# Each batch as one expert's unit: rows out by plain transfers, the routing table only in a branch at the end

## The chip, the cores and the metric

The kernel runs on one core of a Trainium2 chip. Its time is the device time of one execution in microseconds (us). Before the change the median of three runs is 590.32 us (589.46 to 590.48).

## The reference

Three layers, in float32, one behind the other:

```python
# 1. Nystrom attention: 4 batches, 8 heads, 576 tokens, head size 64, 32 landmarks
A, Bm, C = softmax(q k_lm), softmax(q_lm k_lm), softmax(q_lm k)
Z = pseudo-inverse of Bm by six Newton steps
attn = A @ Z @ C @ v                      # -> x[2304, 512], batch by batch
# 2. a dense layer ("moe"): 512 -> 2048 -> 512
h = x @ w_in ; y = (h * clip(h + 3, 0, 6) / 6) @ w_out
# 3. a mixture of 8 experts, one expert for each token, capacity 576 tokens
logits = y @ w_gate ; expert = argmax(logits) ; gate = max of softmax(logits)
# the first 576 tokens of each expert are kept, in order; the others give zero rows
out[token] = gate * (relu(y[token] @ w1[expert]) @ w2[expert])
```

With the inputs of the runs, the reference sends all 576 tokens of batch 0 to expert 2, all of batch 1 to expert 3, and all of batches 2 and 3 to expert 4. Expert 4 is full after batch 2, so the rows of batch 3 are zero.

## The kernel before

**Attention and the dense layer.** Tokens are held in eight blocks of 288, two for each batch. The attention's steps and the first quarter of the dense layer are put in order by hand, by a small planner in the file (class `Order`). The dense layer runs in four quarters of its inner size (`fq` 0 to 3). In each, block after block, `first` multiplies x by a quarter of w_in (six matmuls into ph) and `second` multiplies the result by w_out (twelve matmuls into py). Operands are split into a high and a low part, so that each product is three matmuls. The result y lies transposed in `yacc`: model dimension on the partitions, tokens along the row. The last two blocks (batch 3) get only their logits, by `logits`; their inner values go to DRAM (`r_d`) in case they are needed.

After the first quarter, the order on each engine is that of the framework's scheduler, which works from estimated durations; each engine and each DMA queue then runs its list strictly in order. The loop `moe_rest` goes through (fq, block), in four steps k a block; in each step it emits a `first`, a `second`, one step of the routing (`state["route"]`) and what `side` puts there.

**Routing, in the last quarter.** When a block's y is complete, `route(blk)` runs beside the next blocks: `gate_logits` (8 matmuls), `choose` (the expert of each token as one-hot `oh`, and its gate), then a running count of each expert, and a slot for each token in a table in DRAM, `tab_d` (expert times 2304 plus rank), with token number and gate as its entry. Three indirect DMAs a block on GpSimd's queue write these entries (L898). `turn_y` (L916) transposes y back into rows of tokens, four transposes for 128 rows, ScalarE copies them (L918), and SP's queue writes them to `y_d` (L920).

**The pick.** When both blocks of batch 0 are in the table, `pick` takes the expert with most tokens. SP reads its number into a register and loads its first 576 table entries (`load_idx`, L956 and L957). `gather_first` fetches those rows of y_d by indirect DMA, `turn_first` transposes them and splits them into `xT` (high and low). `w1_first` loads that expert's w1 in four parts and splits it (L994 load, L1000 ScalarE, L1003 VectorE).

**The experts' units.** A unit is up to 576 tokens of one expert. `run_unit` does an up layer (192 matmuls, L1071), and a down layer (96 matmuls on four full blocks of 128 tokens, L1090, and 16 on the last 64 tokens, L1097, which go first). Within the down layer of a unit the next one is prepared: `split1` splits its w1, `turn_rows` (L975) transposes its gathered rows, `fetch2` loads its w2 (L1053). The rows of the result are scaled by the gate and scattered to `out` by indirect DMA on GpSimd's queue (L1107). After unit 0, n_units and n_new are read into registers on all engines; a branch skips `finish_last` (batch 3, L1209), and the other units stand in nested branches (L1211). `out` and batch 3's part of y_d are cleared by writes of zeros in the second quarter (`clear`, L815).

The order of the preparations around the last quarter is one list:

```python
    AHEAD = [(4, 0, gather_first, 0), (4, 0, gather_first, 1), (4, 1, gather_first, 2), (4, 1, gather_first, 3),
             (4, 2, gather_first, 4), (4, 0, w1_first, 0), (4, 2, w1_first, 1), (5, 2, w1_first, 2), (6, 0, w1_first, 3),
             (5, 0, turn_first, 0), (5, 1, turn_first, 1), (5, 2, turn_first, 2), (5, 3, turn_first, 3), (6, 0, turn_first, 4)]
```

The first two numbers are block and step at which the call is emitted.

Of the kernel before, what the change touches and what calls it, by code (L numbers as in the profile page):

```python
# [114 lines left out]
def nystrom_moe_kernel(ctx, tc, qt, kt, v, w_in, w_out, w_gate, w1, w2, capacity, out, dims, dbg=None):  # L115
# [34 lines left out]
    if dbg:  # L150
        y_d, tab_d = dbg
# [24 lines left out]
    for e in range(E):  # L176
# [8 lines left out]
    cnt2 = kp.tile([RT, 2, E], BF16, name="cnt2")  # L185
    nc.gpsimd.memset(cnt2, 0.0)
    cnt_b = cnt2[:, 1, :]
# [3 lines left out]
    below = kp.tile([1, E, UB], F32, name="below")  # L191
    nc.gpsimd.iota(below, pattern=[[0, E], [UNIT, UB]], base=0, channel_multiplier=0,
                   allow_small_or_imprecise_dtypes=True)
    pick_i = kp.tile([1, 3], I32, name="pick_i")
# [6 lines left out]
    idx0 = kp.tile([P, NST, 2], I32, name="idx0")  # L201
    nc.gpsimd.memset(idx0, -1)
# [228 lines left out]
    def moe_rest():  # L431


        while state["todo"]:
            fq, blk = state["todo"].pop(0)
            prev, gh = state["prev"], []
            for k in range(NF):
                if blk < NBLK:
                    emit(first(fq, blk, k, gh))
                if prev and prev[1] < LAST:  # L440
                    emit(second(prev[0], prev[1], k, prev[2]))
                if prev and prev[1] >= LAST and k == 1:
                    logits(*prev)
                if prev and prev[1] >= LAST and k == 2 and prev[0] == NQ - 1:
                    ahead[prev[1]] = choose(lacc[prev[1] - LAST], prev[1])
                next(state["route"], None)
                side(fq, blk, k)
            if prev and prev[0] == NQ - 1:
# [15 lines left out]
    SIDE[1] += [(5, n, "clear", n) for n in range(4)] + [(6, n, "clear", 3 + n) for n in (1, 2)]  # L464
# [338 lines left out]
    ahead = {}  # L803
# [35 lines left out]
    def choose(lt, blk):  # L839
# [6 lines left out]
        sc = mp.tile([RT, 4, RN, 1], F32, tag="sc", name="sc", bufs=4)  # L846
        bc = [RT, RN, E]
        nc.vector.tensor_reduce(sc[:, 0], lg, axis=AX.X, op=ALU.max)
        oh = mp.tile([RT, RN, E], F32, tag="oh", name="oh", bufs=4)
# [8 lines left out]
        ent = mp.tile([RT, RN, 2], I32, tag="ent", name="ent", bufs=4)  # L858
        nc.vector.reciprocal(ent[:, :, 1:2].bitcast(F32), sc[:, 2])
        nc.gpsimd.iota(ent[:, :, 0:1], pattern=[[RT, RN]], base=blk * HB, channel_multiplier=1)  # L860
        ohb = mp.tile([RT, 2, RN, E], BF16, tag="ohb", name="ohb", bufs=4)
        nc.vector.tensor_copy(ohb[:, 0], oh)
        return sc, oh, ent, ohb

    def route(blk):
        if blk < LAST:
            lt = gate_logits(blk)
            yield
            sc, oh, ent, ohb = choose(lt, blk)
        else:  # L870
            sc, oh, ent, ohb = ahead[blk]
        bc = [RT, RN, E]
        if blk == LAST:
            nc.vector.tensor_copy(cnt2[:, 0, :], cnt_b)
        nc.vector.tensor_copy(ohb[:, 1, 0, :], cnt_b)
        for j in range(RN):
            dst = ohb[:, 1, j + 1, :] if j < RN - 1 else cnt_b
            nc.vector.tensor_tensor(dst, ohb[:, 1, j, :], ohb[:, 0, j, :], op=ALU.add)
        yield
        turn_y(blk, 0)  # L880
        if blk < LAST:
            yield
            turn_y(blk, 1)
            turn_y(blk, 2)
        ps = bank([RT, RN, E], "ps_c")
        nc.tensor.matmul(ps, lhsT=upper, rhs=ohb[:, 0], start=True, stop=False)
        nc.tensor.matmul(ps, lhsT=ones_b, rhs=ohb[:, 1], start=False, stop=True)
        t1 = mp.tile([RT, RN, E], F32, tag="t1", name="t1", bufs=4)
        nc.vector.tensor_tensor(t1, ps, oh, op=ALU.mult)
        nc.vector.tensor_reduce(sc[:, 0], t1, axis=AX.X, op=ALU.add)  # L890
        nc.vector.tensor_tensor(t1, oh, base_e[:, None, :].to_broadcast(bc), op=ALU.mult)
        nc.vector.tensor_reduce(sc[:, 1], t1, axis=AX.X, op=ALU.add)
        nc.vector.tensor_tensor(sc[:, 1], sc[:, 1], sc[:, 0], op=ALU.add)
        nc.vector.tensor_scalar(sc[:, 0], sc[:, 0], cap_f, float(E * NT), op0=ALU.is_ge, op1=ALU.mult)
        slot = mp.tile([RT, RN], I32, tag="slot", name="slot", bufs=4)
        nc.vector.tensor_tensor(slot, sc[:, 1, :, 0], sc[:, 0, :, 0], op=ALU.add)  # L896
        for j in range(RN):
            ins = nc.gpsimd.indirect_dma_start(  # L898
                tab_d, bass.IndirectOffsetOnAxis(ap=slot[:, j:j + 1].bitcast(U32), axis=0),
                ent[:, j, :], None, bounds_check=E * NT - 1, oob_is_err=False)  # L900
            for other in placed:
                tc.declare_no_dep(ins.ins, other.ins, reason="every token has a slot of its own")
            placed.append(ins)
        if blk == NBLK // B - 1:
            pick()

    def turn_y(blk, j):

        t = blk % 2 * 2 + j
        n = min(P, S - t * P)  # L910
        if blk >= LAST or blk % 2 == 0 and j == RN - 1:
            return
        t0 = blk // 2 % 2 * S + t * P
        ps = bank([P, KC, P], "ps_r")
        for d in range(KC):
            nc.tensor.transpose(ps[0:n, d, :], yacc[blk // 4][d][:, t0:t0 + n], ident)  # L916
        yr = mp.tile([P, DM], F32, tag="yr", name="yr", bufs=3)
        nc.scalar.activation(yr[0:n, :], ps[0:n].rearrange("p d c -> p (d c)"), AF.Copy)  # L918
        t0 += blk // 4 * 4 * HB
        nc.sync.dma_start(y_d[t0:t0 + n, :], yr[0:n, :])  # L920

    def pick():

        ps = bank([RT, E], "ps_k")
        nc.tensor.matmul(ps, lhsT=ones_b, rhs=cnt_b, start=True, stop=True)
        key = mp.tile([1, E], F32, name="pk", bufs=1)
        nc.vector.scalar_tensor_tensor(key, ps[0:1, :], float(E), rank[:, 0:E], op0=ALU.mult, op1=ALU.add)
        top = mp.tile([1, 8], F32, name="pt", bufs=1)
        nc.vector.max(top, key)
        nc.vector.tensor_copy(pick_i[:, 0:1], top[:, 0:1])  # L930
        nc.vector.tensor_scalar(pick_i[:, 2:3], pick_i[:, 0:1], E.bit_length() - 1, None,
                                op0=ALU.logical_shift_right)
        nc.vector.tensor_scalar(pick_i[:, 0:1], pick_i[:, 0:1], E - 1, None, op0=ALU.bitwise_and)
        nc.vector.tensor_scalar(pick_i[:, 1:2], pick_i[:, 0:1], float(NT), None, op0=ALU.mult)
        ex, sl = (nc.values_load(pick_i[0:1, n:n + 1], engines=[ET.SP], min_val=0, max_val=m,
                                 skip_runtime_bounds_check_because=ON_CHIP) for n, m in ((0, E - 1), (1, (E - 1) * NT)))
        state["ex"] = ex
        load_idx(idx0, sl)
        state["src"] = rows_of(idx0, mp.tile([P, NST], I32, name="src0", bufs=1))

        seen = mp.tile([1, 2], F32, name="seen", bufs=1)
        lead = mp.tile([1, NCAND], F32, name="lead", bufs=1)
        nc.vector.tensor_scalar(seen[:, 0:1], pick_i[:, 0:1], float(UB), None, op0=ALU.mult)
        nc.vector.tensor_scalar(lead, rank, seen[:, 0:1], None, op0=ALU.is_equal)
        nc.vector.tensor_copy(seen[:, 0:1], pick_i[:, 2:3])
        nc.vector.tensor_scalar(seen[:, 1:2], seen[:, 0:1], float(UNIT), float(NT), op0=ALU.is_ge, op1=ALU.mult)
        nc.vector.tensor_tensor(seen[:, 0:1], seen[:, 0:1], seen[:, 1:2], op=ALU.max)
        belowf = below.rearrange("p e u -> p (e u)")
        nc.vector.scalar_tensor_tensor(belowf, lead, seen[:, 0:1], belowf, op0=ALU.mult, op1=ALU.add)

    tail = UNIT - (NST - 1) * P
    xT = [t.rearrange("p g n -> p (g n)").rearrange("p (k n) -> p k n", k=KC) for t in at[0]]

    def load_idx(ti, sl):
        full = (NST - 1) * P
# [301 lines left out]
```

## Time and profile before

| | |
|---|---|
| median of three runs | 590.32 us |
| the profiled execution | 589.89 us, span 588.1 us |
| busy: PE / DVE / ACT / POOL | 565.2 / 302.9 / 306.8 / 252.0 us |
| PE's matmuls of the dense layer (L362, L400) | 133.3 + 160.6 + 114.4 us |
| PE's matmuls of the experts (L1071, L1090, L1097) | 26.9 + 25.8 + 25.7 + 69.5 + 11.0 us |
| PE's last matmul ends | 576.75 us |
| DMA | 71.27 MB |

The engines are named PE (TensorE matmul), PEld (TensorE weight load), DVE (VectorE), ACT (ScalarE), POOL (GpSimd) and SP, whose queue issues most of the DMAs. The ends of matmuls are modelled and overlap, so busy times of PE rows cannot be added up; the distance from one start to the next can.

### The profile page before, as it was taken

The page shows a single profiled execution, that of the slowest core. Times are in us where ns is not written, and L with a number is a line of the kernel's source. Part 1 is how long each engine was busy: PE and PEld are TensorE (multiplying, and loading weights), DVE is VectorE, ACT ScalarE, POOL GpSimd, SP SyncE. Part 2 cuts the span into 40 slices and gives each one's busy share as a digit, 9 for nine tenths or more (in the row PEclk, how much of TensorE's full clock was granted, in tenths as well). Part 3 has the DMA queues.
Part 4 walks back from the last instruction along what each step waited for, and adds up shares of the span by engine and source line. Part 5 has one row for each costly group of instructions (what it writes and reads, how often), then busy time and mean ns, then how long its engine had stood idle before and what let it go on. Part 6 is the DMA issues. An engine that isn't in the chain of part 4 may idle for free. (4 is left out here: it accounts for less than half of the span.)

```text
span 588.1 us, 12087 instructions
## 1 busy us (share of the span) xinstructions
PE 565.2 (96%) x4606; PEld 483.2 (82%) x4606; DVE 302.9 (52%) x837; ACT 306.8 (52%) x706; POOL 252.0 (43%) x287
## 2 busy tenths in 40 slices
PE   8999999999999999999999999899999999999992
PEld 7767678797777999879998899798997797899771
DVE  2779987633555575555655766577642022202120
ACT  3779778654675654456544544454355155343520
POOL 3467647633052532134420012332698275647630
PEclk9999999999999999999999999999999999999997
DMA  7757254004781232112302001543756143416511
GB/s 294 253 191 280 115 194 120 32 1 118 250 270 38 82 99 90 64 37 72 103 17 71 2 37 46 181 134 100 191 191 193 58 162 102 151 54 199 169 47 40
DMA packets 31354, 71.27 MB, mean 121 GB/s; under 512 B 6704, under 2 KB 11312, under 8 KB 31280
## 3 DMA queue, kind: packets, MB, share of 16 engines
q1 hardware_dynamic: 27248, 61.89, 31.7%
q0 software_dynamic: 3392, 8.42, 4.9%
q8 instruction: 40, 0.66, 0.5%
q14 instruction: 34, 0.28, 0.2%
q10 hardware_dynamic: 640, 0.02, 0.1%
HBM read 52.46 MB, written 17.86 MB: 120 GB/s over the span
## 5 line engine op out<-in xcount | busy, mean ns | idle before, releaser
L400 PE MATMUL py<-ghi,wo 128*128 128x288 f32 x768 | 160.6, 301 | 3.1 <-ACT ghi L381 2.1
L362 PE MATMUL ph<-at,vv 128*128 128x288 f32 x768 | 133.3, 309 | 0.1
L400 PEld LDWEIGHTS py<-ghi,wo 128*128 128x128 f32 x768 | 124.3, 189 | 5.7 <-ACT ghi L381 2.3
L362 PEld LDWEIGHTS ph<-at,vv 128*128 128x128 f32 x768 | 108.3, 189 | 20.2 <-issue 17.7
L400 PE MATMUL py<-glo,wo 128*128 128x288 f32 x384 | 114.4, 298 | 0.7 <-DVE glo L385 0.2
L385 POOL TENSOR_TENSOR glo<-r,ghi 128x288 fp32r<-128x288 f32 x72 | 58.2, 810 | 108.0 <-ACT ghi L381 92.4
L371 ACT ACTIVATE r<-ph,half 128x288 f32<-128x288 f32 x128 | 64.0, 500 | 54.8 <-PE ph L362 45.9
L373 DVE SCALAR_TENSOR_TENSOR r<-r,ph 128x288 f32<-128x288 f32 x128 | 57.6, 450 | 43.7 <-ACT r L371 43.2
L400 PEld LDWEIGHTS py<-glo,wo 128*128 128x128 f32 x384 | 72.6, 189 | 1.8 <-POOL glo L385 1.1
L1090 PE MATMUL ps_o<-w2s,hT 128*128 128x512 f32 x288 | 69.5, 395 | 0.0
L1090 PEld LDWEIGHTS ps_o<-w2s,hT 128*128 128x128 f32 x288 | 53.2, 188 | 13.1 <-issue 2.4
L381 ACT ACTIVATE ghi<-r 128x288 fp32r<-128x288 f32 x96 | 42.4, 442 | 38.1 <-DVE r L373 37.7
L1077 DVE SCALAR_TENSOR_TENSOR hT<-ps_h,hT 128x288 fp32r<-128x288 f32 x48 | 21.9, 456 | 78.4 <-ACT hT L1074 51.7
L898 POOL DMA_INDIRECT tab_d<-ent,slot x24 | 22.4, 935 | 83.8 <-DVE slot L896 45.5
L411 DVE TENSOR_TENSOR yacc<-py,yacc 128x288 f32<-128x288 f32 x72 | 32.6, 453 | 18.8 <-PE py L400 18.6
L1074 ACT ACTIVATE hT<-ps_h 128x288 fp32r<-128x288 f32 x48 | 19.6, 408 | 39.9 <-PE ps_h L1071 38.9
L1102 ACT ACTIVATE rows_o<-ps_o,idx 128x512 f32<-128x512 f32 x12 | 8.3, 688 | 46.8 <-PE ps_o L1090 37.3
L1107 POOL DMA_INDIRECT out<-rows_o,idx x15 | 14.7, 982 | 41.0 <-ACT rows_o L1102 26.5
L272 POOL TENSOR_TENSOR wo<-cvt,wo 128x512 fp32r<-128x512 f32 x16 | 20.6, 1288 | 25.1 <-ACT wo L270 25.1
L1037 POOL TENSOR_TENSOR w2s<-raw,w2s 128x512 fp32r<-128x512 f32 x24 | 30.1, 1293 | 1.7 <-ACT w2s L1036 1.7
L726 PE MATMUL pn<-yy 128*128 128x192 f32 (+1 forms) x112 | 28.2, 334 | 0.4 <-DVE st L654 0.2
L1071 PE MATMUL ps_h<-at,vv 128*128 128x288 f32 x192 | 26.9, 297 | 0.0
(268 smaller groups left out, 931.7 us busy)
## 6 DMA issues: line engine op xcount, KB each, us to landing
raw<-in_moe_w SPq DMA_DIRECT2D x12, 1024.0 KB, 6.9
raw<-in_moe_w_in SPq DMA_DIRECT2D x16, 512.0 KB, 6.0
raw<-in_moe_w_out SPq DMA_DIRECT2D x16, 512.0 KB, 3.8
out<-zero SPq DMA_DIRECT2D x6, 768.0 KB, 5.6
r_d<-r SPq DMA_DIRECT2D x32, 144.0 KB, 1.8
vm<-in_v SPq DMA_DIRECT2D x8, 512.0 KB, 7.3
qT<-in_q SPq DMA_DIRECT2D x6, 576.0 KB, 6.9
qT<-in_k SPq DMA_DIRECT2D x6, 576.0 KB, 6.5
```

The source lines that it names most:

```text
L362: nc.tensor.matmul(ph, lhsT=vv[pair][g][a][:, b, f * P:(f + 1) * P], rhs=at[pair][c][:, g, tok], start=n == 0, stop=n == 3 * NG - 1)
L371: nc.scalar.activation(r, ph, AF.Relu, bias=half, scale=1.0 / 6.0)
L373: nc.vector.scalar_tensor_tensor(r, r, 1.0, ph, op0=ALU.min, op1=ALU.mult)
L381: nc.scalar.activation(ghi, r, AF.Copy)
L385: eng.tensor_tensor(glo, r, ghi.bitcast(F32), op=ALU.subtract)
L400: nc.tensor.matmul(py, lhsT=w[a][:, f, d * P:(d + 1) * P], rhs=gh[f][c], start=f == 0 and n == 0, stop=f == NF - 1 and n == 2)
L411: nc.vector.tensor_tensor(y, py, y, op=ALU.add)
L726: nc.tensor.matmul(pn[:, cols], lhsT=yy[:, 0:P], rhs=yy[:, cols], start=True, stop=True)
L898: ins = nc.gpsimd.indirect_dma_start(tab_d, bass.IndirectOffsetOnAxis(ap=slot[:, j:j + 1].bitcast(U32), axis=0), ent[:, j, :], None, bound ...
L1037: nc.gpsimd.tensor_tensor(dst[1], src, dst[0].bitcast(F32), op=ALU.subtract)
L1071: nc.tensor.matmul(ps, lhsT=w1s[i % 2](f // NF, a, kk)[:, fs], rhs=xT[c][:, kk, cols], start=n == 0, stop=n == 3 * KC - 1)
L1090: nc.tensor.matmul(ps, lhsT=hT[a][:, f, cols], rhs=w2s[c][:, f, :], start=n == 0, stop=n == 3 * FC - 1)
```

## The change

Batches 0 to 2 are each taken as one unit, in order of tokens, on the assumption that each batch has chosen one expert. Then the unit's x is the batch's y as it lies, transposed, in `yacc`: it is written to DRAM in that form (`yt_d`) and loaded again for units 1 and 2; for unit 0 it is split straight out of `yacc` (`x_first`). The gates go through DRAM (`gate_d`) to come back with tokens on the partitions. Rows of `out` are contiguous and written by plain DMAs on SP's queue. `count(b)` takes each batch's counts and picks its expert, one register on SP each. `plain` works out whether the assumption holds (each of batches 0 to 2 has one expert, all different, batch 3 goes to one of them, capacity 576). If not, a branch at the very end clears `out`, builds the table, turns y back into rows and runs the general units.

```diff
-    SIDE[1] += [(5, n, "clear", n) for n in range(4)] + [(6, n, "clear", 3 + n) for n in (1, 2)]
+    SIDE[1] += [(5, n, "clear", n) for n in range(2)]
...
-    fill = mp.tile([P, E * NT // P, 2], I32, name="fill", bufs=1)
-    nc.gpsimd.memset(fill[:, :, 0:1], -1)
-    nc.gpsimd.memset(fill[:, :, 1:2], 0)
-    nc.gpsimd.dma_start(tab_d.rearrange("(p n) t -> p n t", p=P), fill)
...
-        parts = [r.rearrange("(p n) d -> p n d", p=RT) for r in (out, y_d[LAST * HB:, :])]
-        for r, k in zip(parts, (NT // RT // 6, S // RT // 6)):
-            nc.sync.dma_start(r[:, n * k:(n + 1) * k, :], zero[0:RT, None, :].to_broadcast([RT, k, DM]))
+        r = out[LAST * HB:, :].rearrange("(p n) d -> p n d", p=RT)
+        k = S // RT // 2
+        nc.sync.dma_start(r[:, n * k:(n + 1) * k, :], zero[0:RT, None, :].to_broadcast([RT, k, DM]))
...
+        nc.vector.reciprocal(prob[:, blk], sc[:, 2])
+        if blk < LAST:
+            nc.sync.dma_start(gate_d[blk * HB:(blk + 1) * HB].rearrange("(j p) -> p j", p=RT), prob[:, blk, :, 0])
+        if blk % 2:
+            count(blk // 2)
 
     def route(blk):
...
+        lt = gate_logits(blk)
+        if blk % 2:
+            for d in range(KC):
+                b = blk // 2
+                nc.sync.dma_start(yt_d[b, d], yacc[b // 2][d][:, b % 2 * S:(b % 2 + 1) * S])
         yield
-        turn_y(blk, 0)
-        if blk < LAST:
-            yield
-            turn_y(blk, 1)
-            turn_y(blk, 2)
-        ps = bank([RT, RN, E], "ps_c")
...
+        choose(lt, blk)
+
+    def count(b):
+
+        part = mp.tile([RT, E], BF16, tag="cnt", name="cnt", bufs=2)
+        sums = mp.tile([RT, E], F32, tag="cnt_f", name="cnt_f", bufs=2)
+        nc.vector.tensor_reduce(sums, chosen[:, 2 * b:2 * b + 2].rearrange("p b j e -> p e b j"), axis=AX.XY, op=ALU.add)
+        nc.vector.tensor_copy(part, sums)
+        ps = bank([RT, E], "ps_k")
+        nc.tensor.matmul(ps, lhsT=ones_b, rhs=part, start=True, stop=True)
+        nc.vector.tensor_copy(tot[:, b, :], ps[0:1, :])
+        if b == B - 1:
             return
...
+        state["ex", b] = nc.values_load(pick_i[0:1, b:b + 1], engines=[ET.SP], min_val=0, max_val=E - 1,
+                                        skip_runtime_bounds_check_because=ON_CHIP)
...
+    def split_x(d, src):
+        nc.scalar.activation(xT[0][:, d, :], src, AF.Copy)
+        nc.vector.tensor_tensor(xT[1][:, d, :], src, xT[0][:, d, :].bitcast(F32), op=ALU.subtract)
+
+    def x_first(d):
+        split_x(d, yacc[0][d][:, 0:S])
...
+    AHEAD = [(4, 0, w1_first, 0), (4, 2, w1_first, 1), (5, 2, w1_first, 2), (6, 0, w1_first, 3),
+             (5, 0, x_first, 0), (5, 1, x_first, 1), (5, 2, x_first, 2), (5, 3, x_first, 3)]
...
         def fetch(i):
...
             for a in range(2):
-                nc.sync.dma_start(raw1[a], w1[bass.ds(ex, 1), a * 2 * P:(a + 1) * 2 * P, :].rearrange(
-                    "o (k p) f -> p (o k) f", p=P))
-            return ex
+                load_w1(state["ex", i], a)
+            nc.sync.dma_start(xraw, yt_d[i].rearrange("k p n -> p k n"))
...
+        def load_gates(i):
+            g = gate_d[i * S:(i + 1) * S]
+            nc.sync.dma_start(gates[i][:, 0:NST - 1], g[0:full].rearrange("(t p) -> p t", p=P))
+            nc.sync.dma_start(gates[i][0:tail, NST - 1:NST], g[full:].rearrange("(t p) -> p t", p=tail))
...
-            nc.gpsimd.indirect_dma_start(out, bass.IndirectOffsetOnAxis(
-                ap=ti[0:r, t, 0:1].bitcast(U32), axis=0), ro[0:r, :], None, bounds_check=NT - 1, oob_is_err=False)
+            put(ro[0:r, :])
 
         def run_unit(i):
-            more = i < NU
+            more = i < B - 2
             if more and i:
-                ex = fetch(i + 1)
+                fetch(i + 1)
+            load_gates(i)
             for f in range(FC):
                 hi, lo = up_layer(i, f)
                 split2(f)
                 if i == 0 and f < 3:
                     with tc.issue_after(hi):
-                        fetch2(state["ex"], (f + 1,), 4)
+                        fetch2(state["ex", 0], (f + 1,), 4)
                 if i == 0 and f == 2:
-                    ex = fetch(i + 1)
-                if more and f == (3 if i else 5):
-                    with tc.issue_after(lo):
-                        src = rows_of(idx[(i + 1) % 2], up.tile([P, NST], I32, name=f"src{i + 1}"))
-                    state["src"] = src
-                    for t in range(NST):
-                        gather(t, rows_x[t], src, NT)
+                    fetch(i + 1)
             for t in range(NST):
-                down_layer(i, NST - 1 - t)
+                k = NST - 1 - t
+                rows = slice(i * S + k * P, i * S + k * P + size(k))
+                down_layer(k, gates[i][0:size(k), k:k + 1], lambda ro: nc.sync.dma_start(out[rows, :], ro))
...
                 if more and t == 1:
-                    turn_rows()
-
-        def turn_rows():
-            for n in range(NST):
-                turn(n, rows_x[n], px_p.tile([P, KC, P], F32, tag="x", name="ps_x"))
+                    for d in range(KC):
+                        split_x(d, xraw[:, d, :])
...
+        redo = up.tile([1, 1], I32, name="redo")
+        plain(redo)
+        fetch2(state["ex", 0], (0,), 4)
+        for i in range(B - 1):
+            run_unit(i)
+        again = nc.values_load(redo, min_val=0, max_val=1, skip_runtime_bounds_check_because=ON_CHIP)
+        with ExitStack() as nest:
+            nest.enter_context(tc.If(again > 0))
+            blank()
+            cnt_b = place()
+            for b in range(B - 1):
+                turn_back(b)
             finish_last()
...
             for i in range(NU):
                 nest.enter_context(tc.If(n_units > i))
-                run_unit(i + 1)
+                general(i, plan)
```

## Rows read from the trace of the kernel before

**Rows 1.** The page's first part: busy us (share of the span) x instructions, for PE.

```profile
PE 565.2 (96%) x4606; PEld 483.2 (82%) x4606; DVE 302.9 (52%) x837; ACT 306.8 (52%) x706; POOL 252.0 (43%) x287
```

**Rows 2.** Waits of PE: engine, line, waited for: us in total, times, longest.

```profile
PE py L400 <- ACT ghi L381: 2.1, 1, 2.1
...
PE ps_h L1071 <- ACTq L1209: 1.2, 1, 1.2
```

**Rows 3.** Windows: busy us of each engine, clock, DMA share, GB/s; last quarter, first unit.

```profile
core 0: us, PE busy (x) PEld busy (x) DVE busy (x) ACT busy (x) POOL busy (x), PEclk, DMA share, GB/s
340.00:412.28 72.28, 68.83 (x532) 63.18 (x529) 49.52 (x220) 35.77 (x79) 20.04 (x26) 0.98 0.32 104
412.28:465.00 52.72, 52.72 (x330) 45.10 (x330) 19.40 (x81) 21.97 (x52) 36.78 (x35) 1.00 0.57 167
```

**Rows 4.** DMA issues: line, engine, count, KB each, median us to landing.

```profile
raw<-in_moe_w SPq DMA_DIRECT2D x12, 1024.0 KB, 6.9
...
y_d<-yr SPq DMA_DIRECT2D x12, 256.0 KB, 2.8
...
idx<-tab_d SPq DMA_DIRECT2D x4, 4.0 KB, 2.0
```

**Rows 5.** Timeline of PE, starts of rounds: start us, us, engine, line, operation.

```profile
300.01 0.95 PE L362 MATMUL ph<-at,vv 128*128 128x288 f32 x6
...
302.40 0.95 PE L362 MATMUL ph<-at,vv 128*128 128x288 f32 x6
...
345.57 1.04 PE L362 MATMUL ph<-at,vv 128*128 128x288 f32 x6
...
348.55 1.04 PE L362 MATMUL ph<-at,vv 128*128 128x288 f32 x6
...
354.47 1.04 PE L362 MATMUL ph<-at,vv 128*128 128x288 f32 x6
...
357.28 1.04 PE L362 MATMUL ph<-at,vv 128*128 128x288 f32 x6
```

**Rows 6.** Groups of PE by shape: count, busy us, mean ns; transposes of turn_rows.

```profile
L975 PE MATMUL ps_x<-ident,rows_x 128*128 128x128 f32 x48 | 6.9, 276 | 0.0
```

**Rows 7.** Timeline of PE: the second unit's down layer, the third's first matmul.

```profile
498.38 5.76 PE L1090 MATMUL ps_o<-w2s,hT 128*128 128x512 f32 x24
...
508.70 14.37 PE L1090 MATMUL ps_o<-w2s,hT 128*128 128x512 f32 x62
522.91 7.31 PE L1071 MATMUL ps_h<-at,vv 128*128 128x288 f32 x54
```

**Rows 8.** Timelines of PE, ACT and SP, and one window, around the pick.

```profile
372.70 1.03 PE L362 MATMUL ph<-at,vv 128*128 128x288 f32 x6
...
378.71 0.69 PE L833 MATMUL pb<-yacc,gate 128*32 128x288 f32 x8
...
383.76 0.49 PE L843 MATMUL pb<-ident,lt 128*96 128x128 f32 x3
384.00 1.04 PE L362 MATMUL ph<-at,vv 128*128 128x288 f32 x6
...
376.48 0.63 ACT L1000 ACTIVATE wo<-raw_e 128x512 fp32r<-128x512 f32 x1 [5.12 <-DMA raw_e<-in_moe_w]
...
370.59 0.43 SPq L956 DMA_DIRECT2D idx<-tab_d  x1
...
372.30 0.88 SPq L994 DMA_DIRECT2D raw_e<-in_moe_w  x2
...
380.00:382.00 2.00, 2.00 (x10) 2.00 (x10) 1.93 (x8) 2.00 (x5) 0.88 (x2) 0.50 0.83 238
```

**Rows 9.** Timeline of PE: the last wait of the routing.

```profile
412.21 0.17 PE L886 MATMUL pb<-ohb,upper 96*96 96x24 bf16 x1 [0.73 <-ACT yr L918]
```

**Rows 10.** Timelines of ACT and POOL: the last eviction and the last scatter.

```profile
576.84 0.69 ACT L1102 ACTIVATE rows_o<-ps_o,idx 128x512 f32<-128x512 f32 x1 [4.75 <-PEq L1211]
...
577.80 0.97 POOL L1107 DMA_INDIRECT out<-rows_o,idx  x1 [4.46 <-ACT rows_o L1102]
```

**Rows 11.** Waits of SP's queue: line, waited for: us in total, times, longest.

```profile
SPq L1053 <- PE ps_o L1097: 54.4, 6, 21.3
```

More of the change, by code (lines that the diff above doesn't have):

```diff
@@ L857, in choose @@
         nc.vector.tensor_scalar(sc[:, 2], sc[:, 2], 1e-9, None, op0=ALU.add)
[L858 to L863, printed above, removed]
-    def route(blk):
-        if blk < LAST:
-            lt = gate_logits(blk)
-            yield
[L869 to L878, printed above, removed]
-        yield
-        turn_y(blk, 0)
-        if blk < LAST:
-            yield
-            turn_y(blk, 1)
-            turn_y(blk, 2)
-        ps = bank([RT, RN, E], "ps_c")
[L886 to L911, printed above, removed]
-            return
[L913 to L928, printed above, removed]
-        nc.vector.max(top, key)
[L930 to L949, printed above, removed]
@@ L1029, in nystrom_moe_kernel @@
         raw1 = [up.tile([P, 2, F2], F32, name=f"raw1{i}") for i in range(2)]
-        rows_x = [up.tile([P, DM], F32, name=f"rows_x{t}") for t in range(NST)]
-        idx1 = up.tile([P, NST, 2], I32, name="idx1")
-        nc.gpsimd.memset(idx1, -1)
-        idx = [idx0, idx1]
+        rx = up.tile([P, NST * DM], F32, name="rx")
+        rows_x = [rx[:, t * DM:(t + 1) * DM] for t in range(NST)]
+        xraw = rx[:, 0:KC * S].rearrange("p (k n) -> p k n", k=KC)
+        gates = [up.tile([P, NST], F32, name=f"gate{i}") for i in range(B - 1)]
         def split(dst, src):
@@ L1079, in up_layer, with down_layer @@
             return hi.ins, lo.ins
-        def down_layer(i, t):
-            ti = idx[i % 2]
+        def down_layer(t, gate, put):
             r = size(t)
@@ L1172, in finish_last, with turn_back @@
                     nc.sync.dma_start(y_d[blk * HB + t:blk * HB + t + n, :], rows_o[1][0:n, :])
+        def turn_back(b):
+            nc.sync.dma_start(xraw, yt_d[b].rearrange("k p n -> p k n"))
             for t in range(NST):
-                gather(t, rows_x[t], state["src"], NT)
-            turn_rows()
-        ps = px_p.tile([RT, 2, E], F32, tag="x", name="ps_n")
-        nc.tensor.matmul(ps, lhsT=ones_b, rhs=cnt2, start=True, stop=True)
-        cnt12 = up.tile([1, 2, E, 1], F32, name="cnt12")
@@ new lines, in general @@
+        def general(i, plan):
+            ex = nc.values_load(plan[0:1, 1, i:i + 1], engines=[ET.SP], min_val=0, max_val=E - 1,
+                                skip_runtime_bounds_check_because=ON_CHIP)
+            sl = nc.values_load(plan[0:1, 2, i:i + 1], engines=[ET.SP], min_val=0, max_val=E * NT - UNIT,
+                                skip_runtime_bounds_check_because=ON_CHIP)
+            nc.sync.dma_start(idx[:, 0:NST - 1, :], tab_d[bass.ds(sl, full), :].rearrange("(t p) c -> p t c", p=P))
+            nc.sync.dma_start(idx[0:tail, NST - 1, :], tab_d[bass.ds(sl + full, tail), :])
+            nc.vector.tensor_scalar(src, idx[:, :, 0], 0.0, None, op0=ALU.max)
+            for a in range(2):
+                load_w1(ex, a)
+            fetch2(ex)
+            for t in range(NST):
+                r = size(t)
+                nc.gpsimd.indirect_dma_start(rows_x[t][0:r, :], None, y_d, bass.IndirectOffsetOnAxis(
+                    ap=src[0:r, t:t + 1].bitcast(U32), axis=0), bounds_check=NT - 1, oob_is_err=False)
+                turn(t, rows_x[t])
+            for kk in range(KC):
+                split1(1, kk)
+            for f in range(FC):
+                up_layer(1, f)
+                split2(f)
+            for t in range(NST):
+                r = size(t)
+                down_layer(t, idx[0:r, t, 1:2].bitcast(F32), lambda ro: nc.gpsimd.indirect_dma_start(
+                    out, bass.IndirectOffsetOnAxis(ap=idx[0:r, t, 0:1].bitcast(U32), axis=0), ro, None,
+                    bounds_check=NT - 1, oob_is_err=False))
```

204 lines of the change are left out of this document (125 added, 79 removed).

## Prediction

> **What bounds the kernel now.** I read the page's busy times first: PE is busy 565.2 of 588.1 us [rows 1]. Then PE's own list of waits: the longest is 2.1 us, the next that matters 1.2 us [rows 2]. So nothing but TensorE's own stream sets the end. What takes an instruction out of that stream moves the end by its place in the stream; what is done on VectorE, ScalarE, GpSimd or by DMA counts only where PE waits for it. In the last quarter of the first MoE (340 to 412 us), where most of the edits fall, DVE is busy 49.5 and ACT 35.8 of 72.3 us [rows 3]: room there, not plenty. I then read PE's order of time around each piece that goes, because the matmuls overlap and a busy time is not a price: the price is start to start.
>
> **What goes from PE's stream.**
> - turn_y: 15 groups of four transposes (12 full and 3 partial blocks of rows, as the writes of y show [rows 4]). A plain round of the last quarter (six ph and twelve py matmuls) is 302.40 - 300.01 = 2.39 us, one with such a group 357.28 - 354.47 = 2.81 [rows 5]. So 0.42 us a group, 6.3 us in all.
> - turn_first: 5 groups of the same shape, 2.1 us at the same price.
> - turn_rows: 15 groups, among the down layer's matmuls (48 of the transposes, in 12 groups, are in one row [rows 6]; three groups are smaller). Between the first full down matmul of the second unit and the next unit's first matmul lie 522.91 - 498.38 = 24.53 us; it holds 96 matmuls of (522.91 - 508.70) / 62 = 0.229 us, 21.98 in all [rows 7]. The other 2.55 us are the five groups. The third unit turns rows for a fourth that never runs, so three times: 7.65 us.
> - The table's count: 8 pairs of small matmuls. A round with one group and one pair is 348.55 - 345.57 = 2.98 us, 0.17 over that with the group alone [rows 5]: 1.4 us. Two single ones (L925, L1179) go and four come in count(): 0.2 back. Net 1.2 us.
>
> **Waits that go.**
> - The pick. PE needs 384.00 - 372.70 = 11.30 us for two rounds [rows 8]. Their content: two plain rounds (4.78), the gate logits (0.69 at most), one turn_first group (0.42, already counted) and three transposes (384.00 - 383.76 = 0.24), 6.13 in all. 5.2 us are lost. The rows show how: idx waits for the table's scatters and is issued at 370.59, the first of w1 at 372.30; ACT has the split of w1 next in its queue and stands 5.12 us until 376.48; ghi is behind it, PE behind ghi [rows 2, 8]. Afterwards TensorE runs at half its clock: 0.50 granted from 380 to 382, that is 1.2 instead of 2.4 GHz [rows 8]. The change takes the expert two steps earlier (in choose, not at the end of route), from the counts alone; no table, no idx. The pick then stands two rounds (2.4 to 2.8 us each [rows 5]) earlier in PE's order, and with the table's wait gone I estimate w1's issue some 10 us before 372.30. What is late next: the four writes of yt (1.2 MB) go ahead of w1 on the same queue; at the 2.8 us of a 256 KB write [rows 4], overlapping, I estimate 4 us. That leaves the load before ACT's place for it. I take all 5.2 us; ends 0 and 5.2.
> - The end of that stage: PE waits 0.73 us for the last yr [rows 9]. It goes: 0.7. Next come the first unit's matmuls, whose x and w1 are split earlier.
> - The branch after the first unit: 1.2 us [rows 2]. The three units are straight code now: 1.2.
> - The end: after the last eviction (576.84 + 0.69) POOL needs until 577.80 + 0.97 = 578.77 for the scatter's descriptors [rows 10]; SP's issue of a plain transfer takes some 0.4 us, by that of idx (0.43) [rows 8]. 0.8 us gained, against a register load and a branch which now stand behind that write: 0 to 1.2 us by the branch wait [rows 2]. I take 0.4; ends -0.4 and 0.8.
>
> **What is added, at nothing, and its cover.**
> - Splitting x by rows of y: 4 ACT copies and 4 DVE subtractions of 128x576 a unit, from SBUF, in place of 5 and 5 of 128x512 from PSUM. With the 15 yr copies of ACT gone and some 60 tiny DVE operations of the table too, both engines get lighter [rows 3]. ACT sets no wait in the down layers, so 4 times about 0.7 us stand beside 24 us of matmuls. Uncovered: 2.8 us a unit, 8.4 in all.
> - SP's queue. It gets 12 yt writes (288 KB each) for 15 y writes, 6 writes and 6 loads of gates in 4-byte pieces (nearest: idx, 8-byte pieces, 2.0 us to landing [rows 4]), two x loads of 1.2 MB, and the 15 row writes that POOL issued; it loses idx and most of the clearing (6 of 768 KB and 6 of 192 KB become two of 576 KB). Moved past it: three register loads, one for each unit, each waiting for DVE's pick; behind them stand r_d writes (7 buffers) and w1. PE waits for none of these before. Bounds: -1 us (less traffic for the conversions) to +5.2 (one more stop like the pick's). I take 0, as no PE wait in the list is for SP.
> - POOL loses 24 scatters, 20 gathers and 15 scatters; its splits of w2 no longer queue behind them. No PE wait rests on them: 0.
>
> **The sum.** 6.3 + 2.1 + 7.65 + 1.2 + 5.2 + 0.7 + 1.2 + 0.4 = 24.75 us. The profiled execution took 589.89 us (span 588.1), so 565.1; the median of the runs is 0.43 above it: 565.5 us.
>
> **Rivals.**
> - A stop like the pick's remains or comes anew: ACT works its list in order, as ghi behind the split showed, the list is fixed ahead from estimated landings, and 1.2 MB of yt or x now share the queue with w1. For it: it happened once here [rows 8]. Against: the chain is two hops shorter. With it 570.7, and with the end and branch terms lost too, 573.
> - Two such stops, or loads late for one unit (w1 and x behind a wait on SP): some 10 us: 575 to 580.
> - Slower: SP becomes the one queue for everything the units need and give, and it is in order. Before, it stood 54.4 us in six waits for raw2, up to 21.3 at a time [rows 11], with nothing urgent behind. If the w1 and x loads of units two and three fall behind such a wait, each unit starts after 6.9 + 6.9 us of w1 [rows 4] and about 8 us of x, exposed: twice 22, so 565.5 + 44 = 609 us. It decides from 12.4 us a unit on (24.75 / 2). Against: the loads stand in program order ahead of w2's, with a whole unit's 50 us to land. The Trainium skill, page "DMA: Bandwidth & Descriptors", section "Anatomy of one DMA — SWDGE (gpsimd) path", has the rule behind this: a DMA's semaphore wait is held on the issuing sequencer, not in the DMA engines, so a waiting issue stops every later one of its engine. The trace agrees, as the wait stands on SP's queue. By the rule alone the row writes and loads would queue behind w2's wait, 609 at worst; without it 565.5.
> - It doesn't do what it says: the branch is taken. Then the three units run again with gathers, at least 3 x 52.7 us (the first unit's window [rows 3]): 565.5 + 158, over 720 us. It is taken when a batch's tokens choose more than one expert. Against: the kernel before runs three units for three batches and turns rows three times [rows 6]; and by the reference, batches 0 to 2 of the inputs go whole to experts 2, 3 and 4, and batch 3 to expert 4 again.
>
> **How the numbers follow.** Forecast (560 to 569) 0.62; one stop (569 to 574) 0.20; two stops or a late load (574 to 588) 0.10; SP blocks, slower 0.04; branch taken 0.01; more than I count 0.03: the 20 transposes among ph and py at 0.51 as in the down layer (2.55 / 5) give 1.8 more, and less DMA traffic 1, so 562.7, and below 560 only with something unseen. The range 560 to 574 leaves out 0.18. Faster by over 0.2% (1.2 us, about what can be told from no change here) 0.94, within it 0.01, slower 0.05.
>
> **What the profile after would show.** No transposes of y or x in PE's stream, only those of the logits; three units' down layers of 22.0 us plus the tail with no gap between units; PE clock 1.00 through the last quarter and no wait of ACT on raw_e; row writes on SP's queue; the last matmul's end 24 us before 577. Wrong would be: a PE wait over 1 us on xT, w1 or hT, a clock of 0.50 anywhere before the end, POOL scatters in the units, or groups of transposes that cost PE less than 0.42 us because the weight loads, not the matmuls, set the pace.

## The result and the profile after

| | before | after |
|---|---|---|
| median of four runs | 590.14 us (589.46 to 590.48) | 571.85 us (566.87 to 572.95) |
| profiled execution | 589.89 us, span 588.1 | 566.87 us, span 565.1 |
| first matmul of the first down layer | 439.71 us | 431.12 us |
| PE's last matmul ends | 576.75 us | 558.84 us |

The ratio is 0.967 [0.962, 0.972]: faster. The median lies 18.3 us under that of before, the profiled execution, the shortest of the four, 23.0 us; the forecast was 24.75. One execution of the changed kernel (751 us) and one of before (3062 us) among the runs below were in a slow state and are left out of every figure. The time is inside the range of 560 to 574, but the median is not where the forecast had it (560 to 569): it is in the stretch of the rival "one stop like the pick's remains" (569 to 574).

The profiled execution splits at the two marks of the table. PE's timelines show the first one, in before and in after:

```profile
439.71 3.65 PE L1097 MATMUL ps_o<-raw,h_tail 128*64 128x512 f32 x16
```

```profile
431.12 3.65 PE L1007 MATMUL ps_o<-raw,h_tail 128*64 128x512 f32 x16
```

| stretch | forecast gain | measured |
|---|---|---|
| to the first down layer (turn_y, turn_first, count, pick, edge) | 15.5 | 439.71 - 431.12 = 8.6 |
| down layers and branch (turn_rows 7.65, branch 1.2) | 8.85 | 17.91 - 8.59 = 9.3 |
| behind the last matmul | 0.4 | (588.1 - 576.75) - (565.1 - 558.84) = 5.1 |
| sum | 24.75 | 23.0 |

Two errors of opposite sign, then, some 7 us and some 5 us, and a middle that holds. The first part of the page of after (as [rows 1]) shows what left: PE is busy 17.7 us less, POOL 69 us less.

```profile
PE 547.5 (97%) x4452; PEld 467.6 (83%) x4452; DVE 286.0 (51%) x737; ACT 293.7 (52%) x675; POOL 183.2 (32%) x205
```

The chain of work that ended last in after (start, duration, what) is PE alone through the units: each down layer takes 22.0 us, where 24.53 stood [rows 7], and the next unit's first matmul begins where the last one of the unit before ends. No transposes and no branch are left there.

```profile
431.19 3.58 PE ps_o L1007 x16
434.77 22.01 PE ps_o L1000 x96
456.78 25.43 PE ps_h L982 x192
482.22 3.58 PE ps_o L1007 x16
485.80 22.00 PE ps_o L1000 x96
507.80 25.43 PE ps_h L982 x192
533.24 3.58 PE ps_o L1007 x16
536.82 22.02 PE ps_o L1000 x96
```

The list of PE's waits of after (as [rows 2]): the branch wait (1.2) and the wait for yr [rows 9] are gone, the long one on ghi is still there.

```profile
PE py L395 <- ACT ghi L376: 2.3, 1, 2.3
...
PE py L395 <- DVE yacc L406: 0.9, 1, 0.9
```

What makes ghi late is the splits of w1, as before [rows 8]. ACT's timeline of after has them (start, duration, operation, in brackets the idle time before it and its releaser):

```profile
366.98 0.63 ACT L909 ACTIVATE wo<-raw_e 128x512 fp32r<-128x512 f32 x1 [3.29 <-DMA raw_e<-in_moe_w]
...
384.84 0.63 ACT L909 ACTIVATE wo<-raw_e 128x512 fp32r<-128x512 f32 x1 [4.55 <-DMA raw_e<-in_moe_w]
...
390.91 0.63 ACT L909 ACTIVATE wo<-raw_e 128x512 fp32r<-128x512 f32 x1 [3.69 <-DMA raw_e<-in_moe_w]
```

SP's timeline of after shows that this is no late issue: the first of w1 goes out at 359.87 us, 12.4 earlier than before [rows 8]; some 10 were forecast.

```profile
345.74 0.32 SPq L850 DMA_DIRECT2D gate_d<-prob  x1
...
356.49 0.32 SPq L850 DMA_DIRECT2D gate_d<-prob  x1
359.87 0.97 SPq L903 DMA_DIRECT2D raw_e<-in_moe_w  x2
...
372.24 0.38 SPq L850 DMA_DIRECT2D gate_d<-prob  x1
373.78 0.32 SPq L859 DMA_DIRECT2D yt_d<-yacc  x1
376.25 0.34 SPq L903 DMA_DIRECT2D raw_e<-in_moe_w  x1
379.96 0.32 SPq L850 DMA_DIRECT2D gate_d<-prob  x1
381.44 0.34 SPq L903 DMA_DIRECT2D raw_e<-in_moe_w  x1
```

It is a slow landing. The answers for the tile raw_e (w1 as it arrives) of before, then of after; the first line of each says who waited (us, times):

```profile
  ACT wo L1000: 5.5, 2
...
DMA to landing us min/median/max: 3.7/3.9/4.9
```

```profile
  ACT wo L909: 11.8, 4
...
DMA to landing us min/median/max: 7.1/7.7/9.4
```

The windows of after (columns as in [rows 3]) show the DMA engines 65 to 97% busy where they move 33 to 55 GB/s, and then the stop: PE is busy 0.58 and 1.12 us of two 2-us windows, and the granted clock falls to 0.50, that is 1.2 of 2.4 GHz.

```profile
360.00:365.00 5.00, 5.00 (x43) 4.37 (x42) 2.22 (x6) 1.83 (x4) 0.00 (x0) 1.00 0.65 33
375.00:380.00 5.00, 5.00 (x40) 5.00 (x39) 4.29 (x19) 2.85 (x7) 0.00 (x0) 1.00 0.97 55
384.00:386.00 2.00, 0.58 (x5) 0.35 (x3) 0.11 (x1) 1.02 (x2) 0.00 (x0) 1.00 1.16 209
386.00:388.00 2.00, 1.12 (x3) 0.59 (x3) 2.00 (x8) 0.83 (x2) 0.00 (x0) 0.79 0.35 12
388.00:390.00 2.00, 2.00 (x12) 1.06 (x12) 0.59 (x2) 0.00 (x0) 0.00 (x0) 0.50 0.46 150
```

By starts of rounds on PE, the stops cost 3.57 - 2.39 = 1.2 us (367.24 to 370.81) and 10.10 - 5.64 = 4.5 us (382.43 to 392.53, where two plain rounds, the gate logits and three transposes take 4.78 + 0.62 + 0.24): 5.6 us.

At the end the last eviction starts at 558.91 us and the program is over 6.19 us later; before, 588.1 - 576.84 = 11.3. There the engines run the program's last instructions, which the profile lists under the kernel's last line (L1253 before, L1274 after). One of them is a DRAIN on GpSimd's queue: at 582.3 us it took 4971 ns before, and the longest of three took 93 ns after (min/median/max in ns, first and last start in us).

```profile
L1253 POOLq DRAIN  x1: 4971/4971/4971, 582.3 to 582.3; - x1
```

```profile
L1274 POOLq DRAIN  x3: 40/50/93, 514.6 to 564.9; - x3
```

### The profile page after: what moved, and what is told of

Its sections match the earlier page's. It is cut to its first block, busy times and chain, and to the rows that moved or that the text cites. A ratio compares the mean times of both kernels' runs of the same rounds, so it can differ in the third digit from the quotient of the medians.

```text
span 565.1 us, 11331 instructions
## 1 busy us (share of the span) xinstructions
PE 547.5 (97%) x4452; PEld 467.6 (83%) x4452; DVE 286.0 (51%) x737; ACT 293.7 (52%) x675; POOL 183.2 (32%) x205
## 2 busy tenths in 40 slices
DMA packets 27886, 59.70 MB, mean 106 GB/s; under 512 B 6576, under 2 KB 11184, under 8 KB 27824
## 4 chain that ended last, share of the span: by engine, by line
PE 79%; DMA 5%; DVE 5%; issue 5%; ACT 3%; POOL 1%; SPq 0%; POOLq 0%; ACTq 0%; DVEq 0%
PE py L395 21%; PE ph L357 14%; PE ps_h L982 14%; PE ps_o L1000 12%; DMA raw_e<-in_moe_w 3%; PE pn L721 3%; PE ps_f L538 2%; PE pb L336 2%; PE ps_o L1007 2%; PE ps_v L336 1%; POOL glo L380 1%; PE pw L704 1%; DMA cap_i<-in_moe_capacity 1%; PE pb L573 1%; DMA raw<-in_moe_w_out 1%
## 5 line engine op out<-in xcount | busy, mean ns | idle before, releaser
L357 PE MATMUL ph<-at,vv 128*128 128x288 f32 x768 | 131.7, 307 | 0.1
L1000 PE MATMUL ps_o<-w2s,hT 128*128 128x512 f32 x288 | 66.2, 391 | 0.0
L1011 ACT ACTIVATE rows_o<-ps_o,gate 128x512 f32<-128x512 f32 x12 | 8.3, 690 | 41.6 <-PE ps_o L1000 39.2
L982 PEld LDWEIGHTS ps_h<-at,vv 128*128 128x128 f32 x192 | 25.7, 188 | 0.7 <-issue 0.7
L982 PE MATMUL ps_h<-at,wo 128*128 128x288 f32 x192 | 25.8, 294 | 0.0
```

Source lines behind the costliest of these rows:

```text
L357: nc.tensor.matmul(ph, lhsT=vv[pair][g][a][:, b, f * P:(f + 1) * P], rhs=at[pair][c][:, g, tok], start=n == 0, stop=n == 3 * NG - 1)
L982: nc.tensor.matmul(ps, lhsT=w1s[i % 2](f // NF, a, kk)[:, fs], rhs=xT[c][:, kk, cols], start=n == 0, stop=n == 3 * KC - 1)
L1000: nc.tensor.matmul(ps, lhsT=hT[a][:, f, cols], rhs=w2s[c][:, f, :], start=n == 0, stop=n == 3 * FC - 1)
```

## Experiments

The theory after the result: the six gate writes, 288 pieces of 4 bytes each, keep the DMA engines at work, so w1 lands late and ACT stands at its split; the stretch at the end was GpSimd's drain after the scatters. The rivals: the yt writes ahead of w1 do it; the queue does it; ACT's order alone does it; any GpSimd transfer costs the drain. The kernel before took 590 us on the chips of the result and of e5 to e8, and 600 on those of e1 to e4 and of e9 to e12, while after took 572 on one of either kind; so variants of after are compared with after by their medians, also across chips. One mark, the start of the first down layer, says nearly all: from it to the end of the span are 134.0 us in after and 134.0 to 134.3 in every variant of after but e8, whose end was changed.

**e1: the changed kernel again.**

> The changed kernel once more, for the spread of its executions and a second trace. Theory (gate writes): executions spread over 567 to 573 us, and the longer ones lose their time between 355 and 407 us, where ACT stands for the load of w1 (3.3 + 4.6 + 3.7 us in the first trace) and PE behind it; the rest of the time is as before to 0.5 us. Rival (yt writes): the same spread, same place. Rival (something in the units or at the end): a longer execution would have a PE wait there or a longer stretch after PE's last matmul (6.3 us in the first trace).

Median 572.36 us (566.69 to 573.0), ratio 0.951 [0.947, 0.954]. The profile is of the execution of 566.69, with w1 landing after 6.9/7.5/9.1 us. So 567 is the short case, seen once in each of the two sets, and 572 the usual one.

**e2: no gates.**

```diff
-            nc.sync.dma_start(gate_d[blk * HB:(blk + 1) * HB].rearrange("(j p) -> p j", p=RT), prob[:, blk, :, 0])
...
-            g = gate_d[i * S:(i + 1) * S]
-            nc.sync.dma_start(gates[i][:, 0:NST - 1], g[0:full].rearrange("(t p) -> p t", p=P))
-            nc.sync.dma_start(gates[i][0:tail, NST - 1:NST], g[full:].rearrange("(t p) -> p t", p=tail))
+            nc.gpsimd.memset(gates[i], 1.0)
```

> Leaves out the gates: neither written to DRAM nor loaded, the rows are scaled by 1. Theory (six gate writes of 288 pieces of 4 bytes fill the DMA engines for 6.6 to 12 us each, and w1's loads behind them land after 7.1 to 9.4 us instead of 3.9): landing of w1 back to about 4 us, no stop of ACT over 1 us on it, no stretch at half clock in the last quarter, 5 to 6 us less than the fastest execution of the changed kernel, 561 us, and a spread under 1 us. Rival (the 1.2 MB of yt on the same queue): w1 still lands after 6 us or more, the stops stay, 566 to 572. Rival (the order of ACT's list alone): w1 lands after 4 us but a stop of 2 us or more stays, 564 or more.

561.22 us (560.9 to 561.86), ratio 0.934 [0.931, 0.936]: 11 us under after, and the spread of 6 us is gone with it. The tile raw_e again:

```profile
  ACT wo L907: 0.8, 1
...
DMA to landing us min/median/max: 3.3/3.6/4.3
```

The first down layer starts at 425.27, so the first stretch gains 14.4 of the forecast's 15.5. The gates' transfers are the cause; writes or loads, and by what means, is left to e5, e9 and e10. The windows tell what they do: from 360 to 365 us the DMA engines are 74% busy here and move 267 GB/s, against 65% and 33 GB/s in after.

**e3: batch 0's yt left out** (no unit reads it).

```diff
-        if blk % 2:
+        if blk % 2 and blk > 1:
             for d in range(KC):
                 b = blk // 2
```

> Leaves out the four yt writes of batch 0, which only the branch at the end would read. Theory (gate writes): w1 still lands after 7 us or more, within 1.5 us of the changed kernel. Rival (yt writes): these four writes are the ones in front of the first w1 loads; without them landing at about 4 us, the first stop (3.3 us of ACT) gone, 1.5 to 3 us less.

572.25 us (568.86 to 572.97), w1 landing after 7.0/7.5/12.7: no different from after. This rival falls for batch 0; the other yt writes stay here, but they stay in e2 too, where w1 is not late. The profile is of an execution of 572.97 us and shows what the usual, long one is: the last w1 part comes so late that ACT stands 8.24 us (3.69 in after's profile), PE's list of waits has 5.3 us behind it, and the clock is at 0.50 when it goes on. ACT's timeline, PE's waits and the windows of e3:

```profile
394.42 0.63 ACT L909 ACTIVATE wo<-raw_e 128x512 fp32r<-128x512 f32 x1 [8.24 <-DMA raw_e<-in_moe_w]
```

```profile
PE pb L833 <- ACT lt L826: 5.3, 1, 5.3
```

```profile
392.00:394.00 2.00, 0.00 (x0) 0.00 (x0) 0.00 (x0) 0.00 (x0) 0.00 (x0) 0.74 0.41 149
394.00:396.00 2.00, 0.60 (x4) 0.58 (x4) 0.92 (x2) 1.32 (x3) 0.00 (x0) 0.50 0.25 96
```

**e4: the gates moved on the chip**, by matmuls with a shifted unit matrix, nine one-column products a batch.

```diff
-            nc.sync.dma_start(gate_d[...], prob[:, blk, :, 0])
...
+            nc.tensor.matmul(ps[:, t:t + 1], lhsT=wide[:, RT - off:RT - off + P], rhs=prob[:, 2 * b + c // RN, c % RN, :],
+                             start=c == mine[0], stop=c == mine[-1])
+        nc.vector.tensor_copy(gates_k[:, b, :], ps)
```

> The whole computation, with the gates moved to their partitions on the chip: nine matmuls of one column for each batch with shifted unit matrices, one copy, no gate in DRAM. Theory (gate writes): as without gates, plus 27 one-column matmuls (by ps_k's 0.15 to 0.4 us in the stream, 2 to 4 us in all unless they run together): 562 to 565 us, spread under 1 us, faster than both kernels. Rival (yt writes or ACT's order): 568 to 575, the stops stay and the matmuls come on top.

571.69 us (568.4 to 573.3): missed. The load was mended (w1 lands after 3.2/3.6/5.3 us, ACT stands 1.8 us at it), but the nine products are 18 instructions and take 2.15 us in PE's own stream for each of the first two batches; those of the third stand in pieces among other matmuls. The clock fell too: it averaged 0.83 from 380 to 390 us, where PE was busy 9.90 us and the second batch's products stand, but stayed at 1.00 around the first batch's. What made it fall is not separated. PE's timeline and the windows of e4:

```profile
356.34 2.15 PE L873 MATMUL pb<-prob,wide 96*128 96x1 f32 x18
...
380.65 2.15 PE L873 MATMUL pb<-prob,wide 96*128 96x1 f32 x18
```

```profile
350.00:360.00 10.00, 9.88 (x81) 9.08 (x80) 5.50 (x26) 3.76 (x9) 0.00 (x0) 1.00 0.02 9
...
380.00:390.00 10.00, 9.90 (x69) 9.10 (x68) 5.33 (x19) 3.39 (x7) 0.00 (x0) 0.83 0.19 67
```

**e5: the gates written in rows.** One transpose of all gates [96 x 18] at batch 2, one copy, one write of 18 pieces of 384 bytes; the loads stay in 4-byte pieces.

```diff
-            nc.sync.dma_start(gate_d[...], prob[:, blk, :, 0])
+    def send_gates():
+        ps = bank([(B - 1) * S // RT, RT], "ps_gr")
+        nc.tensor.transpose(ps, prob[:, 0:LAST].rearrange("p b j o -> p (b j o)"), ident[0:RT, 0:RT])
+        gt = mp.tile([(B - 1) * S // RT, RT], F32, name="gt", bufs=1)
+        nc.scalar.activation(gt, ps, AF.Copy)
+        nc.sync.dma_start(gate_d.rearrange("(c p) -> c p", p=RT), gt)
```

> The whole computation: the six gate writes of 4-byte pieces become one transpose of the 96 x 18 gates, one copy and one write of 18 pieces of 384 bytes; the gate loads stay as they are. Theory (gate writes): landing of w1 about 4 us as without gates, no stop, 561 to 562.5 us, spread under 1 us; faster than both kernels. Rival (the gate loads in 4-byte pieces matter too): w2 or w1 of the units land late, PE waits over 1 us in the first unit, 564 or more. Rival (any PE work near the stage's end costs more than itself, as the one-column matmuls did): 565 or more.

562.53 us (561.75 to 563.28), ratio to before on its chip 0.952 [0.951, 0.954]; by medians 0.984 of after, and all of the computation is there. w1 lands after 3.5/4.0/4.5 us; ACT still stands 2.1 us at it, with no wait of PE behind, and the spread is 1.5 us where under 1 was expected. So it is the writes, not the loads: these stay, and in after they are issued from 406.19 us on, behind all of w1.

That it is the pieces and not the bytes does not follow from e5 alone, which changes two things: its one write is in longer pieces, and it is issued at 400.38 us, behind all of w1's loads (360.94 to 381.16), where three of after's six writes stand beside them. A write in rows beside the loads was not tried. For the pieces speak the windows named at e2, and that four yt writes of 288 KB issued between the loads of e2 (from 362.41 us) leave w1 at 3.3 to 4.3 us. DMA issues of after, then of e5 (KB each, median us to landing):

```profile
raw_e<-in_moe_w SPq DMA_DIRECT2D x4, 512.0 KB, 7.7
...
gate_d<-prob SPq DMA_DIRECT2D x6, 1.1 KB, 8.3
```

```profile
raw_e<-in_moe_w SPq DMA_DIRECT2D x4, 512.0 KB, 4.0
...
gate_d<-gt SPq DMA_DIRECT2D x1, 6.8 KB
```

The Trainium skill, page "DMA: Bandwidth & Descriptors", section "Rules for kernel authors", says that a last dimension which is strided is turned into one descriptor per element, and to make it contiguous. The profiles agree: after has 6576 packets under 512 B and e2 2928, and of the 3648 between them the elements of the six writes and six loads would be 3456. 1.1 KB in such elements took 8.3 us to land, twice what 512 KB take in e5.

**e6: before, on e5's chip.**

> The kernel before once more, for a trace of the executions of 600 us that it has shown since. Theory (its stop at w1's load and the half clock behind it have no fixed length): the extra 10 us lie between 340 and 420 us, as longer or more stops of ACT or PE there. Rival (another place): they lie in the first 340 us, in the units or after PE's last matmul.

591.93 us, clock 0.989, the shape of before: nothing on the 600 us.

**e7: before with plain row writes on SP** (the rows of units 2 and 3 change places).

```diff
-            nc.gpsimd.indirect_dma_start(out, bass.IndirectOffsetOnAxis(
-                ap=ti[0:r, t, 0:1].bitcast(U32), axis=0), ro[0:r, :], None, bounds_check=NT - 1, oob_is_err=False)
+            row = min(i, B - 1) * S + t * P
+            nc.sync.dma_start(out[row:row + r, :], ro[0:r, :])
```

> The kernel before with one part of the change alone: a unit's rows go out by plain writes on SP's queue, batch after batch, instead of scatters on GpSimd's. Theory (the 11.35 us after PE's last matmul hold GpSimd's drain of its last scatter, 5 us at the program's end): that stretch falls to about 6.5 us, as in the changed kernel (6.3), and the time by 4 to 5 us. Rival (the stretch is the nested branches' jumps): it stays at 10.5 to 11.5 us and the time falls by 0.8 us at most.

584.89 us against 590.48, ratio 0.991 [0.989, 0.992]: 5.6 us. From the last eviction (577.54) to the end are 6.4 us. A long drain is still there, but it starts at 562.8 us and is over while matmuls still run (to 577.5).

```profile
L1253 POOLq DRAIN  x1: 3746/3746/3746, 562.8 to 562.8; - x1
```

**e8: after, with the last unit's rows as plain writes on GpSimd's queue.**

```diff
-    lambda ro: nc.sync.dma_start(out[rows, :], ro))
+    lambda ro: (nc.gpsimd if i == B - 2 else nc.sync).dma_start(out[rows, :], ro))
```

> The changed kernel with the last unit's five row writes as plain writes on GpSimd's queue. Theory (drain of GpSimd's queue at the end after any late DMA of it): the stretch after PE's last matmul grows from 6.3 to about 11 us, the time by 4 to 5 us. Rival (only indirect DMAs cost that): it grows by 1 us at most.

572.52 us, from the last eviction (559.40) to the end 6.9 us, 0.7 more than in after; longest drain 474 ns. A plain transfer on GpSimd's queue does not bring the drain back. The long drains are in the kernels with indirect transfers (before, e7); no run took these out of before and left the rest, so what makes the drain long is open.

```profile
L1274 POOLq DRAIN  x3: 44/107/474, 564.8 to 566.0; - x3
```

**e9: after, with ACT's part of every split of w1 held in program order**, so that none stands early in ACT's list. The writes stay.

```diff
-                if n == 0:
-                    tc.keep_in_program_order(ins)
+                tc.keep_in_program_order(ins)
```

> The changed kernel with all of w1's splits on ACT kept where the program puts them, three steps behind their loads (before, only every other one was), the gate writes as they are. Theory (a late load costs only where ACT has its split early in its list): w1 still lands after 7 us or more, the ACT stops of 3 to 8 us mostly go, 561 to 564 us, small spread. Rival (the load comes so late, or the DMA engines are so filled, that something else stops): 567 to 573 with the same spread.

562.44 us (561.8 to 565.42, a wider spread than e5's), ratio 0.935 [0.930, 0.940]. w1 lands as late as in after, and nobody on ACT waits for it:

```profile
  DVE vv L911: 1.6, 2
...
DMA to landing us min/median/max: 6.8/7.7/8.6
```

So two things had to meet: a load slowed by the small writes, and a split that stands in ACT's list ahead of ghi. Either one taken away gives 562.

**e10: the gate writes on ACT's queue.**

```diff
-            nc.sync.dma_start(gate_d[...], prob[:, blk, :, 0])
+            nc.scalar.dma_start(gate_d[...], prob[:, blk, :, 0])
```

> The changed kernel with the six gate writes issued on ACT's queue instead of SP's, w1's loads still on SP's. Theory (the small pieces fill the 16 engines whatever queue they come from): w1 lands after 6 us or more, 566 to 573. Rival (only what stands behind them in the same queue waits): w1 lands after about 4 to 5 us, the stops go, 561 to 564.

572.67 us (571.93 to 574.8); w1 lands after 6.5/7.8/12.3 us, ACT stands 15.5 us at it. The queue is not the cause. The same page and section of the Trainium skill says that spreading DMAs over issuing engines does not help bandwidth, since all run on the same 16 DMA engines; the 7.8 us beside after's 7.7 agree.

**e11: e5 with turn_y's 15 groups put back** (its transposes, copies and writes of y).

```diff
+        yield
+        turn_y(blk, 0)
+        yield
+        turn_y(blk, 1)
+        turn_y(blk, 2)
```

> The kernel with gates sent as one row write (562.5 us), and turn_y put back as it was: 15 groups of four transposes, their copies on ACT and writes of rows, used by nothing. Prediction's price: 15 x 0.42 = 6.3 us, so 568.8. Rival (part of the 0.42 was the cost of interrupting a round at all, which stays where logits or counts interrupt it anyway): 0.35 a group, 5.2 us, 567.7. Rival (ACT and DVE get so full that PE waits): over 570.

568.88 us (568.54 to 569.26), 6.35 over e5, which ran on another chip; by the two profiles the first down layer starts 433.00 - 427.26 = 5.7 us later. The prediction's term is 6.3.

**e12: before, on a chip where it takes 600.**

> The kernel before once more, for a trace of an execution of 600 us, which it showed on one chip and not on the other. Theory (its stop at w1's load and the half clock behind it have no fixed length): if it takes 600 us, the extra 10 us lie between 340 and 420 us; if it takes 590 again, nothing is told.

599.85 us. Not a longer stop at w1: ACT stands 5.4 us there, 5.5 before. The theory missed: of the 9.9 us by which the first down layer starts later (449.59 against 439.71), 2.8 lie before the first unit's matmuls (415.07 against 412.28) and 7.1 in its up layer. The wait for yr [rows 9] is 1.9 instead of 0.73 us, and in the middle of the first unit's up layer PE stands four times with no releaser that the profile shows, and the clock falls behind it (0.83 from 430 to 440 us). PE's waits and a window of e12:

```profile
PE ps_h L1071 <- issue: 3.5, 4, 1.7
PE pb L886 <- ACT yr L918: 1.9, 1, 1.9
```

```profile
420.00:430.00 10.00, 7.06 (x50) 6.48 (x48) 3.39 (x22) 0.53 (x2) 6.55 (x9) 0.99 0.67 176
```

Why this happens on some chips and not on others stays open.

## Why the prediction was right, and where it was not

**What bounds the kernel.** Right: PE's stream and the few waits in it account for everything up to the last matmul. From the first down layer on, all variants of after run in step.

**What goes from PE's stream.** Right, term by term where it was tested: turn_y 6.35 us by medians, 5.7 by the profiles (e11), for 6.3; turn_rows and the branch 9.3 for 8.85. With the stops out of the way (e2) the first stretch gains 14.4 for 15.5. Some 1.1 us too much was forecast there; which of turn_first, count and edge it is was not tested.

**The pick.** This step failed. The prediction took all of 5.2 us, with 0 as its other end, and the other end is what came: the stop of before went and one of 5.6 us came at the same load, in the profiled execution; in the usual one a second stop makes 5 to 6 us more. Half of the step was right: w1 is issued 12.4 us earlier. The failed half was "edits added at nothing": the gate writes were put at nothing by the nearest row, idx, 8-byte pieces, 2.0 us to landing [rows 4]. That row is a load, of 512 entries of 8 bytes, and stood for writes of 288 elements of 4 bytes; these take 7.5 to 10.4 us to land (the 6.6 to 12.1 in e2's expectation take in the gate loads). Why the larger number of entries landed sooner is open. What matters more, the prediction asked only how long the writes take and not what they do to the transfer behind them. It had put 4 us on the yt writes, which do nothing here (e2, e3). The rival "one stop remains or comes anew" named the place rightly (ACT's list in order, fixed ahead from estimated landings; e9 shows this half) and had the median's time, 570.7; its cause (yt or x on w1's queue) was wrong.

**The end.** Mis-sized: 0.4 was taken, within -0.4 to 0.8; it measured 5.1. The prediction followed the last scatter's data to the end of its descriptors and put a plain issue in its place. The span of before went on for 9 us behind that, which it did not ask about; the drain in it is 4.97 us. e7 gains it without the rest of the change, and e8 shows that plain transfers on the same queue do not cost it.

**The other rivals.** SP's queue blocks nothing: no gap between units. The branch is not taken. What was to show the forecast wrong did show it: the clock of 0.50 before the end, and ACT's waits on raw_e, both at the step that failed.

**The sum.** The two errors nearly cancel in the profiled execution (-5.6 - 1.1 at the stage, +4.7 at the end, +0.5 in the down layers: 24.75 becomes 23.2, measured 23.0), so its agreement with 565.1 is luck in part. By medians they do not cancel, 18.3 us for 24.75, and the time is in the range only because the range took in one such stop. Without either error, 24.75 + 4.7 = 29.4 us from the median of 590.14: 560.7, and e2, which has neither gates nor stops, took 561.2.

## What to carry to other kernels

Price a write in small pieces by the load that runs beside it, not by its bytes, and from a row of its own kind: here six writes of 1.1 KB cost 9 us by medians (571.85 - 562.5) because large loads behind them landed 4 us later, and the nearest row, a load of 8-byte entries, said nothing of it. A late load cost time only where an in-order engine had its consumer listed ahead of something urgent (e9), so there are two cures, and either is worth nearly all: list the consumer later (562.4 us), or gather the pieces into one write behind the loads (562.5 us). And follow the last engine's row to the end of the span: what lies behind the last data is time too.

## What the runs showed of the hardware

- The kernels with indirect transfers had a drain of 5.0 and 3.7 us on GpSimd at the end of its list (before, e7); without them it was 0.09 us, with plain transfers on the same queue 0.47 us (after, e8).
- Writes of 288 elements of 4 bytes took 7.5 to 10.4 us to land, and 512 KB loads beside them landed after 7.7 us (median) instead of 3.6 without the gates (e2), from SP's and from ACT's queue alike.
- In e4 the granted clock averaged 0.83 over 10 us of which PE was busy 9.90: a stretch with 2.15 us of one-column products. The same products 24 us earlier left it at 1.00, so the cause is open.
- One and the same kernel, before, took 590 us on some chips and 600 on others, while after took 572 on one of either kind.
